# Loading q and k in token order with casting transfers and turning them with transfer transposes, in an attention and mixer kernel

## The chip, the cores and the metric

The program runs on one core of one Trainium2 chip. The metric is the device time of one execution in microseconds (us). Each kernel was timed in several executions beside the kernel before on the same chip. All executions were of the fast state but one of the kernel before in the second call (323.0 us); the medians quoted from that call contain it, ratios and means do not. Differences "of the means" are between fast runs. A ratio is the mean time of one kernel's fast runs over the mean of the other's from the same rounds, so it is not quite the ratio of the medians that are quoted with it. "Stretch" below means the time from the first matmul of one batch's dense part to that of the next batch's. In the profile's lines PE, DVE, ACT and POOL are TensorE, VectorE, ScalarE and GpSimd, PEld is TensorE's loading of weights, and SP is SyncE, which issues transfers (a q after a name is an engine's instruction queue). A "piece" is one packet of a transfer; "the dense part" is the pair of large layers at the end of the reference below.

## The reference, cut to what matters

```python
# q, k, v: (8 batches, 8 heads, 576 tokens, 64), float32; 8 global tokens
scores = scale * np.matmul(q, k.transpose(0, 1, 3, 2))
# kept: |i - j| <= 32, or i or j global
attn = exp(scores - max) / sum
x = (attn @ v)                                   # as (B, S, H * D)
h = relu(x^T @ w_tok1) @ w_tok2;  u = x + h^T     # token mixing
out = u + relu(u @ w_ch1) @ w_ch2                # dense part, 512 -> 1536 -> 512
```

q and k are drawn with a factor of 0.1. A score is 64 products of about 0.01, divided by 8, so of the order of 0.01, and the attention weights are nearly uniform. A kernel that uses another batch's q and k still passes the comparison. By the same token, passing it says little about whether the changed kernel's new layouts are right.

## The kernel before: the parts that the change touches

The scores need q and k with the head dimension on the partitions, two heads stacked to 128 rows. They come from memory with tokens on the partitions. The kernel before loads them as float32, casts them on ScalarE, turns them on TensorE against an identity matrix, and copies them from PSUM on VectorE:

```python
def qk_src(ten, b, hs):              # 4 tokens = 1 KB per piece
    return ten[b, hs, 0 : S - LAST, :].rearrange("h (p i) d -> p h (i d)", i=4)
def cast_qk(b, ti, p, eng): ...      # float32 -> float16, ScalarE
def T(b, p, at="m"):                 # 8 transposes for a pair of heads
    for ti, n in enumerate((qn, kn)):
        for i in range(4):
            nc.tensor.transpose(out=pT[:, ti, P * i : P * i + P], in_=n[b % 2][:, i, 2 * p : 2 * p + 2, :], identity=ident)
def TEq(b, p, ...): ...              # PSUM -> query layout, VectorE; TEk the same for keys
def TR(b, at="m"): ...               # the last 64 tokens: 16 small selection matmuls; TRE copies them
```

Each batch's dense part (384 + 372 large matmuls in all, in "units" written D) is interleaved by a hand-made word list with the attention of the next two batches: in the list of batch b, `n` is batch b+1, `m` is b+2, `o` is b+3. So the layouts of batch 3 are made during the dense part of batch 1, and so on. Each engine is given its instructions in the order of the words.

The softmax here doesn't subtract the row's maximum and nothing guards it: scores larger than these inputs give would overflow.

## Time and profile before

| | before |
|---|---|
| median | 318.32 us (316.93 to 320.08, 4 runs) |
| TensorE busy | 302.7 of 318.2 us |
| stretches from batch 2 on | 32.27, 37.62, 32.28, 37.62 us, TensorE busy throughout |
| pieces moved by the transfers | 78,407 |

The page's first part gives busy time by engine and the second shows it over 40 slices. The chain that ended last says what the end depended on. While an engine that works in order never rests, its list of work is the time, and the other engines are slack. The prediction shows these lines.

### The profile page before, as it was taken

The numbers are of one execution on the slowest core, as the hardware profiler recorded it, in microseconds if no ns is written. First come the engines' busy times: TensorE is split into PE (matmuls) and PEld (weight loads), VectorE is DVE, ScalarE is ACT, GpSimd is POOL, SyncE is SP. The second block draws the span as 40 slices with busy tenths as digits, with TensorE's granted clock in tenths as the row PEclk, the third lists the DMA queues.
The fourth block names the chain that finished last, engine by engine and source line by source line (L and its number), as shares of the span: only waits on it lengthen the run. The fifth ranks groups of instructions, "written<-read, shape, count | busy, mean of one in ns | idle before, by whom it ended". The sixth has DMA issues, their size and how long they took to land.

```text
span 318.2 us, 8333 instructions
## 1 busy us (share of the span) xinstructions
PE 302.7 (95%) x3555; PEld 168.3 (53%) x3555; DVE 192.0 (60%) x425; ACT 155.7 (49%) x281; POOL 60.8 (19%) x93
## 2 busy tenths in 40 slices
PE   3989799998999999999999999999999999999993
PEld 1457655556467546554657455555556455444643
DVE  7477746869956896667665756658755753321022
ACT  3471469435884427644765427553765404405500
POOL 5796448330041003100310005000000000000000
PEclk9999989999999999999999999999999999999998
DMA  7899999993689939971997119971103130231022
GB/s 218 226 137 260 253 190 185 238 169 99 238 65 248 175 103 113 204 162 63 138 201 188 69 70 117 269 117 68 52 3 65 68 103 2 49 116 52 0 99 68
DMA packets 78407, 41.83 MB, mean 131 GB/s; under 512 B 54498, under 2 KB 72610, under 8 KB 78370
## 3 DMA queue, kind: packets, MB, share of 16 engines
q0 software_dynamic: 38528, 12.85, 33.2%
q1 hardware_dynamic: 39840, 28.45, 32.0%
q8 instruction: 28, 0.46, 0.6%
q14 instruction: 9, 0.07, 0.1%
q10 hardware_dynamic: 2, 0.00, 0.0%
HBM read 36.04 MB, written 9.44 MB: 143 GB/s over the span
## 4 chain that ended last, share of the span: by engine, by line
PE 90%; DVE 5%; ACT 2%; DMA 1%; issue 1%; SPq 0%; DVEq 0%; ACTq 0%
PE op L845 29%; PE b1p L819 27%; PE a1p L721 5%; PE pT L426 4%; PE hp L744 4%; PE s L482 4%; PE b1lp L832 3%; PE pv L678 3%; PE pv L687 3%; PE warm L238 1%; DMA out_dram<-osb 1%; PE pr L453 1%; PE og L558 1%; PE a1p L635 1%; DVE kT L438 1%
## 5 line engine op out<-in xcount | busy, mean ns | idle before, releaser
L822 ACT ACTIVATE b<-b1p 128x512 f16<-128x512 f32 x96 | 57.3, 599 | 74.7 <-PE b1p L819 73.6
L819 PE MATMUL b1p<-uT,wc 128*128 128x512 f16 x384 | 92.9, 383 | 0.0
L845 PE MATMUL op<-wc,b 128*128 128x512 f16 x372 | 85.9, 380 | 0.0
L819 PEld LDWEIGHTS <-wc 128*128 128x128 f16 x384 | 35.6, 99 | 38.0 <-issue 1.1
L845 PEld LDWEIGHTS <-b 128*128 128x128 f16 x372 | 34.3, 98 | 39.4
L387 POOL DMA_DIRECT2D vsh<-in_v_dram x35 | 29.4, 851 | 124.0 <-DVE rr L707 105.7
L492 ACT ACTIVATE e_all<-s 128x544 f16<-128x544 f32 (+1 forms) x64 | 40.1, 685 | 20.8 <-PE s L482 15.5
L849 DVE TENSOR_TENSOR osb<-u,op 128x512 f32<-128x512 f16 x31 | 21.2, 685 | 41.1 <-PE op L845 41.0
L432 DVE COPY qT<-pT 128x512 f16<-128x512 f16 x30 | 20.5, 685 | 12.7 <-PE pT L426 12.7
L755 DVE TENSOR_TENSOR u<-x,hp 128x1024 f16<-128x1024 f16 x14 | 17.0, 1220 | 13.5 <-PE hp L744 13.5
L503 DVE TENSOR_TENSOR e_all<-e_all,bandm 128x616 f16<-128x616 f16 x56 | 24.4, 476 | 1.0
L708 DVE TENSOR_TENSOR x<-pv,rr 128x512 f16<-128x512 f32 x35 | 24.2, 692 | 1.2
L438 DVE COPY kT<-pT 128x512 f16<-128x512 f16 x30 | 20.4, 683 | 5.7 <-PE pT L426 5.2
L412 ACT CAST kn<-lk 128x512 f16<-128x512 f32 x27 | 16.5, 617 | 3.8 <-DMA lk<-in_k_dram 3.8
L678 PE MATMUL pv<-rf,lf 128*64 128x264 f16 x140 | 18.1, 279 | 0.0
L412 ACT CAST qn<-lq 128x512 f16<-128x512 f32 x27 | 16.4, 615 | 3.1 <-DMA lq<-in_q_dram 3.1
L687 PE MATMUL pv<-vsh,e_all 128*64 128x66 f16 x336 | 17.9, 194 | 0.0
L687 PEld LDWEIGHTS <-e_all 128*64 128x64 f16 x560 | 17.2, 111 | 0.0
L482 PEld LDWEIGHTS <-kT 64*64 64x64 f16 x704 | 10.8, 107 | 11.7 <-issue 8.3
L482 PE MATMUL s<-qT,kT 64*64 64x136 f16 (+2 forms) x704 | 15.2, 215 | 1.1 <-ACT e_all L492 0.7
L744 PE MATMUL hp<-a,w 128*128 128x512 f16 x58 | 14.8, 379 | 0.0
L687 PE MATMUL pv<-vod,e_all 128*64 128x66 f16 x224 | 14.5, 194 | 0.0
(183 smaller groups left out, 353.0 us busy)
## 6 DMA issues: line engine op xcount, KB each, us to landing
out_dram<-osb SPq DMA_DIRECT2D x31, 256.0 KB
lq<-in_q_dram SPq DMA_DIRECT2D x5, 1024.0 KB
lk<-in_k_dram SPq DMA_DIRECT2D x5, 1024.0 KB
wc<-in_moe_w_ch_dram POOLq DMA_DIRECT2D x6, 512.0 KB
vsh<-in_v_dram POOLq DMA_DIRECT2D x21, 128.0 KB
lq<-in_q_dram POOLq DMA_DIRECT2D x2, 1024.0 KB
lk<-in_k_dram POOLq DMA_DIRECT2D x2, 1024.0 KB
vsh<-in_v_dram POOLq DMA_DIRECT2D x14, 96.0 KB
```

The lines of the kernel that those rows point to most:

```text
L387: nc.gpsimd.dma_start(out=vsh[b % 2][r0:r1, c, :, 0:D], in_=v[b, :, j0 : j0 + (r1 - r0), :].rearrange("h p d -> p h d"),)
L412: eng(out=(qn, kn)[ti][b % 2][:, :, hs].rearrange("p i h d -> p h i d"), in_=(lq, lk)[ti][:, hs])
L482: nc.tensor.matmul(ps[o, par, i0 - a : i1 - a], lhsT=kT[r, HQ * j : HQ * j + HQ], rhs=qf[r, i0:i1], start=b > 0, stop=b > 0 or j in js[-2:],)
L492: nc.scalar.activation(out=e2[:, :, a:z], in_=ps[:, :, 0 : z - a], func=AF.Exp, scale=scale)
L503: nc.vector.tensor_mul(out=e2[:, par], in0=e2[:, par], in1=bm)
L678: nc.tensor.matmul(ps[r0 : r0 + 64, hf, 0 : NP * VW], lhsT=s["lf"][:, HQ * t : HQ * t + HQ], rhs=s["rf"][:, 2 * g : 2 * g + 2], start=True ...
L687: nc.tensor.matmul(ps[r0 : r0 + 64, hf, VW * hh : VW * hh + VW], lhsT=e_all[:, h, lo : lo + HQ], rhs=(vod if t % 2 else vsh)[b % 2][:, tau ...
L708: nc.vector.tensor_tensor(out=x16s[b % 2][r, tau, :].rearrange("p (f h x) -> p f h x", f=2, h=NP), in0=pq[r, :, :, 0:D], in1=rr[r].unsquee ...
L744: nc.tensor.matmul(ps[:, i, :], lhsT=w2[:, ch, P * tau : P * tau + P], rhs=s["a1"][:, ch, :], start=(ch == 0), stop=(ch == 1),)
L819: nc.tensor.matmul(ps, lhsT=wc1[:, cc, P * j : P * j + P], rhs=s["uT"][:, cc, :], start=(cc == 0), stop=(cc == 3))
L822: nc.scalar.activation(out=s["b1"][:, j, :], in_=ps, func=AF.Relu)
L845: nc.tensor.matmul(ps, lhsT=w, rhs=wc2[:, j, :], start=(j == 0), stop=(j == NJ - 1))
```

## The change

For batches 3 to 7 the four steps become two transfers. GpSimd issues loads that cast to float16 in token order; SyncE issues transposes from SBUF straight into the layouts that the scores read. The padding before each query tile grows from 8 to 16 columns, for all batches; the prediction gives the reason, the alignment of the transposes' destination.

```diff
-QS = P + NG
+QS = P + Q0          # Q0 = 16
+    zq, zk = [const.tile([P, NT, H, D], F16, name=f"z{n}") for n in "qk"]
+    def load_z(b, ti, c):
+        n = P if c < NT - 1 else LAST
+        nc.gpsimd.dma_start(
+            out=(zq, zk)[ti][0:n, c], in_=(q, k)[ti][b, :, P * c : P * c + n, :].rearrange("h p d -> p h d")
+        )
+    def turn_z(b, ti, c):
+        dst = qTs[b % 2][:, :, c, Q0 : Q0 + n] if ti == 0 else kTs[b % 2][:, :, WIN + P * c : WIN + P * c + n]
+        nc.sync.dma_start_transpose(out=dst, in_=(zq, zk)[ti][0:n, c].rearrange("p h d -> p (h d)"))
...  (NG becomes Q0 wherever a query tile is addressed; the whole word list is rewritten:
...   for batches 3 to 7 the words CQ CK R r T Q K LQ go, Z = load_z and Y = turn_z come)
```

More of the change, by code (lines that the diff above doesn't have):

```diff
@@ L18 @@
 NG = 8
+Q0 = 16
 WIN = 32
 GW = 2 * NG
-QS = P + NG
+QS = P + Q0
 HQ = 64
@@ L27 @@
     """
-    nCQ.2 nR.v D nCK.3 nT.0.1 D D D nCK.2 nGL nK.0 D D nQ.0 nT.1.1 nr D D D nCQ.3 nQ.1 mLP nS.0.0.0 nK.1 nS.0.1.1 nT.2.v
-    nX.0.0 nQ.2 nX.0.1 nM.0 D D nS.1.1.1 nK.2 nS.1.0.0 nX.1.0 nX.1.1 mLV nT.3.m D nS.2.1.1 nQ.3 nK.3 nM.1 nS.2.0.0
-    nX.2.0 nX.2.1 nGK.v nLX nM.2 nLM nVO nS.3.0.0 nS.3.1.1 D nX.3.1 nX.3.0 D nM.3 D nOG.0 nRF D nPV.0.v nNO.0 mCK
-    nPV.1.0 nPV.3.1 nNO.1 D mCQ.2 nPV.2.0 mCQ.1 nNO.3 nNO.2 nPV.4.v nNO.4 nA.0.1 mCK.0 nA.1.1 D mGL nA.2.1 mCQ nA.3.1
-    nA.4.1 nRU mCQ.0 D mR.m mCQ.3 mr nH.0.v nH.1.1 nAD.0 nAD.1 D mCK.3 nP.0 mT.0.0 nUT.0 mCK.1 mQ.0 mK.0 mT.1.m mK.1
@@ L33 @@
-    nP.1 mCK.2 nUT.1 mS.0.0.0 mS.0.1.1 mT.2.m mQ.1 mQ.2 mX.0.0 mX.0.1 mK.2 mM.0
-    """,
-    """
-    nT.3.v nQ.3 nS.1.0.0 nS.1.1.1 mLQ nX.1.0 nX.1.1 D nK.3 D nS.2.1.1 nS.2.0.0 nX.2.0 nX.2.1 D nM.1 D nGK.1 nVO nLX
-    nS.3.0.0 nM.2 nS.3.1.v nX.3.0 nLM nX.3.1 D D nM.3 nOG.1 D D nRF nPV.0.v.h mCQ.1 mCK.1 nNO.0 nPV.2.0 bAT mCK mCK.0
-    nPV.1.1 D mCQ.0 bU.2 D bHL nNO.1 D nNO.2 mCQ.3 nA.0.1 nA.1.1 nA.2.1 nPV.3.v mCQ nNO.3 nPV.4.0 mCQ.2 mR.m nNO.4 mCK.3
-    D mCK.2 mr nA.3.1 nA.4.1 mT.0.v nRU mK.0 bGC D D mLV nH.1.0 mQ.0 oLQ mT.3.v nAD.1 nH.0.1 D D nAD.0 nU.0 mGL mT.1.0
@@ L40 @@
-    mK.1 mQ.1 mT.2.1 mK.2 mQ.2 D mS.0.1.0 D mQ.3 mS.0.0.1 mX.0.1 mS.1.0.0 mK.3 D mX.0.0 nU.1 mS.2.0.1 mS.2.1.v mX.1.0
-    mS.1.1.0 mX.1.1 D bGT.0 mVO mX.2.1 mX.2.0 mM.0 D mS.3.1.1 mX.3.1 mS.3.0.v D mM.1 mX.3.0 bGE mM.3 mM.2 D D mOG.1
-    mGK.0 mLX mRF mLM D
-    """,
-    """
-    D nPV.0.v.h nNO.0 bAT nPV.1.1 nNO.1 nPV.2.0 nNO.2 mCQ mCK mCQ.0 D mCK.0 D D nA.0.1 nA.1.1 nA.2.1 mCQ.1 mCK.1 mR.m mr
-    nPV.3.v nNO.3 nPV.4.0 nNO.4 mCQ.2 mCK.2 D D nA.3.1 mT.0.v mQ.0 mK.0 mCQ.3 D nA.4.1 nRU mCK.3 mT.1.0 mQ.1 mK.1 mLV
@@ L47 @@
-    mGL oLQ D D nH.0.1 nAD.0 nU.0 D nH.1.0 nAD.1 nU.1 mT.2.v mQ.2 mK.2 D mT.3.1 mQ.3 mK.3 D D mS.0.0.1 mX.0.0 mS.0.1.0
-    mX.0.1 mS.1.0.v mX.1.0 D mM.0 D mS.1.1.0 mX.1.1 mS.2.0.1 mX.2.0 mS.2.1.v mX.2.1 D mM.1 D mM.2 mS.3.0.0 mX.3.0
-    mS.3.1.1 mX.3.1 mVO mM.3 D D mGK.v mLX mLM mOG.0 mRF D
-    """,
-    """
-    D nPV.0.v.h nNO.0 bHL bAT bU.2 nPV.1.1 nNO.1 nPV.2.0 nNO.2 mCQ mCK mCQ.0 D mCK.0 D D nA.0.1 nA.1.1 nA.2.1 mCQ.1
-    mCK.1 mR.m mr nPV.3.v nNO.3 nPV.4.0 nNO.4 mCQ.2 mCK.2 D D nA.3.1 mT.0.v mQ.0 mK.0 mCQ.3 D nA.4.1 nRU mCK.3 mT.1.0
@@ L54 @@
-    mQ.1 mK.1 mLV mGL oLQ D D nH.0.1 nAD.0 nU.0 D nH.1.0 nAD.1 nU.1 mT.2.v mQ.2 mK.2 D mT.3.1 mQ.3 mK.3 D D D D mS.0.0.1
-    mX.0.0 mS.0.1.0 mX.0.1 mS.1.0.v mX.1.0 D mM.0 D mS.1.1.0 mX.1.1 mS.2.0.1 mX.2.0 mS.2.1.v mX.2.1 D mM.1 D mM.2
-    mS.3.0.0 mX.3.0 mS.3.1.1 mX.3.1 mVO mM.3 D D mGK.v mLX mLM mOG.0 mRF D
+    D D D nR.0 D nr nGL D nT.0.v nQ.0 nCK.2 D D nK.0 nCQ.2 D nT.1.v nK.1 nQ.1 nCQ.3 nCK.3 mLP D nS.0.0.0 mLV nS.0.1.1
+    nX.0.1 nX.0.0 D nT.2.v nQ.2 nK.2 D nS.1.0.0 nX.1.0 nM.0 nS.1.1.1 nX.1.1 nT.3.v D nK.3 nM.1 nS.2.0.0 nS.2.1.1 nX.2.0
@@ new lines @@
+    nX.2.1 nQ.3 D nM.2 nVO nGK.v nLX nLM nS.3.0.0 nX.3.0 nS.3.1.1 nX.3.1 D nM.3 D nOG.v nRF nPV.0.v nPV.1.1 nNO.0 nNO.1
+    D mCQ nPV.2.v nNO.2 nPV.3.1 D nNO.3 mCK mCQ.2 nA.0.0 mCQ.0 nPV.4.1 mCQ.3 nNO.4 mCK.0 mCK.1 mCQ.1 mR.m mr nA.1.0
+    nA.2.0 nA.3.0 nA.4.0 nRU mCK.3 mCK.2 D mGL D nH.0.v nAD.0 nH.1.0 nAD.1 D nP.0 nUT.0 mT.0.m nP.1 mQ.0 mK.0 mT.1.m
+    mK.1 mS.0.0.0 nUT.1 mS.0.1.1 mX.0.0 mX.0.1 mT.2.m mQ.1 mQ.2 mK.2 mM.0
+    """,
+    """
+    mZ.0.1 mZ.1.0 mZ.1.2 mZ.0.4 nT.3.v nS.1.0.0 mZ.0.2 mZ.1.1 nX.1.0 nS.1.1.1 mZ.1.3 nQ.3 D nX.1.1 nK.3 D mZ.0.3 mZ.0.0
@@ new lines @@
+    mZ.1.4 D nS.2.1.1 nX.2.1 nS.2.0.0 nX.2.0 nM.1 nVO D nGK.v nLX nM.2 nS.3.0.0 nX.3.0 nS.3.1.1 nLM nX.3.1 D nM.3 D
+    nOG.0 nRF D D nPV.0.v.h bHL bAT nPV.2.0 bU.2 nPV.1.1 nNO.0 mY.0.2 mY.0.3 mY.0.1 nNO.1 D mY.1.2 nNO.2 mY.0.0 D D
+    nA.0.1 nPV.3.v nNO.3 nPV.4.0 nNO.4 mY.1.1 D nA.1.1 nA.2.1 D nA.3.1 mY.1.4 nA.4.1 mY.1.0 mY.0.4 nRU D mLV mY.1.3 D
+    mGL nH.0.1 nAD.0 D nU.0 nH.1.0 nAD.1 nU.1 D D bGC bGT.0 bGE oZ.1.2 mS.1.0.v mX.1.0 D mS.0.0.1 mS.0.1.0 oZ.0.2 oZ.0.1
+    oZ.1.0 mX.0.0 oZ.1.1 oZ.0.4 oZ.0.0 oZ.0.3 mX.0.1 oZ.1.3 D mS.1.1.0 mX.1.1 mM.0 mS.2.0.1 mX.2.0 mS.2.1.v mM.1 mX.2.1
@@ new lines @@
+    D mS.3.0.0 mX.3.0 mS.3.1.1 oZ.1.4 mX.3.1 D mM.2 mVO mM.3 D D mOG.0 mGK.v mLX mLM mRF D
+    """,
+    """
+    D nPV.0.v.h nPV.1.1 nNO.0 mY.0.0 nNO.1 nPV.2.0 nNO.2 mY.0.2 bAT mY.0.3 D D nA.0.1 mY.1.2 nA.1.1 mY.1.4 mY.0.4 D
+    nA.2.1 mY.1.3 nPV.3.v mY.1.1 nPV.4.0 mY.0.1 mY.1.0 nNO.3 D nA.3.1 D nNO.4 nA.4.1 nRU D D mLV nH.0.1 D nAD.0 nU.0 mGL
+    D D nH.1.0 oZ.0.0 D D mS.0.0.1 oZ.0.3 nAD.1 mS.0.1.0 mX.0.1 mS.1.0.v mX.0.0 nU.1 oZ.0.1 oZ.0.2 oZ.0.4 oZ.1.1 mM.0 D
+    D oZ.1.4 mS.2.0.1 mS.1.1.0 oZ.1.0 mX.1.0 mS.2.1.v D mX.2.0 oZ.1.3 oZ.1.2 mX.2.1 mX.1.1 mM.1 D mM.2 mS.3.0.0 mS.3.1.1
@@ new lines @@
+    mX.3.1 mVO mX.3.0 mM.3 D D mGK.v mLX mOG.1 mRF mLM D
+    """,
+    """
+    D bHL mY.1.0 nPV.1.1 nNO.1 nPV.2.0 nPV.0.v.h nNO.0 mY.0.0 mY.0.1 bAT nNO.2 mY.1.1 D mY.0.2 bU.2 D D nA.0.1 nPV.3.v
+    mY.0.3 nNO.3 mY.1.2 nPV.4.0 mY.0.4 nA.1.1 nA.2.1 mY.1.3 mY.1.4 nNO.4 D D nA.3.1 D nA.4.1 nRU D mLV D nH.0.1 mGL D
+    nAD.0 nU.0 D nH.1.v D nAD.1 nU.1 D D D oZ.0.0 mS.0.0.1 mX.0.0 mS.0.1.0 mX.0.1 mS.1.0.v oZ.0.4 D oZ.0.1 mX.1.0 mM.0 D
+    oZ.0.2 oZ.0.3 mS.1.1.0 mX.1.1 mS.2.0.1 mX.2.0 mS.2.1.v mX.2.1 oZ.1.0 oZ.1.1 oZ.1.3 D mS.3.0.0 mX.3.0 mVO mM.1
@@ L57 @@
+    mS.3.1.1 D mM.2 D mX.3.1 oZ.1.2 mM.3 D mGK.v oZ.1.4 mOG.0 mRF D mLX mLM
     """,
@@ L188, in qk_pads @@
         nc.vector.memset(kTs[i][:, :, WIN + S :], 0.0)
+        nc.vector.memset(qTs[i][:, :, :, 0:Q0], 0.0)
     qk_pads(0)
-    nc.vector.memset(qTs[0][:, :, :, 0:NG], 0.0)
     nc.vector.memset(lv[0:WIN, 0], 0.0)
@@ L303 @@
     for rs, cs, base, sg in ((slice(0, P), 0, 64, 1), (slice(0, P), 0, 0, -1), (slice(0, HQ), 1, 0, 1), (slice(HQ, P), 1, 0, -1)):
-        o = b3[rs, :, NG + HQ * cs : NG + HQ * cs + HQ]
+        o = b3[rs, :, Q0 + HQ * cs : Q0 + HQ * cs + HQ]
         nc.gpsimd.affine_select(
@@ L390, in load_v16 @@
             )
+    def load_z(b, ti, c):
[4 more added lines that the diff above has]
+    def turn_z(b, ti, c):
+        n = P if c < NT - 1 else LAST
+        dst = qTs[b % 2][:, :, c, Q0 : Q0 + n] if ti == 0 else kTs[b % 2][:, :, WIN + P * c : WIN + P * c + n]
+        nc.sync.dma_start_transpose(out=dst, in_=(zq, zk)[ti][0:n, c].rearrange("p h d -> p (h d)"))
     def load_qk1(b=1):
@@ L418, in globals_ @@
         nc.vector.tensor_copy(
-            out=qTs[b % 2][:, :, :, 0:NG], in_=gT[:, b].unsqueeze(2).to_broadcast([P, NP, NT, NG])
+            out=qTs[b % 2][:, :, :, Q0 - NG : Q0], in_=gT[:, b].unsqueeze(2).to_broadcast([P, NP, NT, NG])
         )
@@ L432, in TEq @@
         eng(
-            out=qTs[b % 2][:, p, 0:4, NG:QS].rearrange("p t (x i) -> p t x i", i=4),
+            out=qTs[b % 2][:, p, 0:4, Q0:QS].rearrange("p t (x i) -> p t x i", i=4),
             in_=st[b]["pT", p][:, 0].rearrange("p (i t x) -> p t x i", i=4, t=4),
@@ L460, in TRE @@
             v_ = st[b]["pr"][:, ti].rearrange("p i (n x) -> p n x i", n=NP)
-            dst = qTs[b % 2][:, :, NT - 1, NG : NG + LAST] if ti == 0 else kTs[b % 2][:, :, WIN + 512 : WIN + S]
+            dst = qTs[b % 2][:, :, NT - 1, Q0 : Q0 + LAST] if ti == 0 else kTs[b % 2][:, :, WIN + 512 : WIN + S]
             eng(out=dst.rearrange("p n (x i) -> p n x i", i=4), in_=v_)
     def qcol(t):
-        return QS * (t // 2) + (NG + HQ) * (t % 2) if t >= 0 else 0
+        return QS * (t // 2) + (Q0 + HQ) * (t % 2) if t >= 0 else 0
     def S_(b, p, part, at=None):
@@ L477, in S_ @@
             i0 = max(qcol(j - 1), a)
-            i1 = min(qcol(j) + HQ + NG * (j % 2 == 0), z)
+            i1 = min(qcol(j) + HQ + Q0 * (j % 2 == 0), z)
             o = slice(HQ * (j % 2), HQ * (j % 2) + HQ)
@@ L496, in SM @@
         if b > 0:
-            gc = bass.AP(tensor=e2.tensor, offset=e2.offset, ap=[e2.ap[0], [QS, NT], [ES, 2], [1, NG]])
+            gc = bass.AP(tensor=e2.tensor, offset=e2.offset + Q0 - NG, ap=[e2.ap[0], [QS, NT], [ES, 2], [1, NG]])
             nc.vector.tensor_tensor(
@@ L534, in GK @@
             o = ps[32 * p : 32 * p + 32]
-            qv = qTs[b % 2][:, p, :, NG:QS]
+            qv = qTs[b % 2][:, p, :, Q0:QS]
             w = kgz[:, b, p, :]
@@ L598, in PV0 @@
             tau = t // 2
-            lo = QS * tau + (NG + HQ if t % 2 else NG)
+            lo = QS * tau + (Q0 + HQ if t % 2 else Q0)
             for par in range(2):
@@ L685, in local @@
                 h = NP * (hf ^ sw) + hh
-                lo = QS * tau + (NG + HQ if t % 2 else NG)
+                lo = QS * tau + (Q0 + HQ if t % 2 else Q0)
                 nc.tensor.matmul(
@@ L1023 @@
         H=M2, AD=AD, HL=HL, AT=AT, U=M3, P=M3p, UT=UT, VO=v_odd, GL=globals_, LV=load_v16, LQ=lambda b: (load_rest(b), load_qk(b, slice(0, H))),
-        LP=load_qk1, CQ=lambda b, p=None: cast_qk(b, 0, p, A), CK=lambda b, p=None: cast_qk(b, 1, p, A),
+        LP=load_qk1, Z=load_z, Y=turn_z, CQ=lambda b, p=None: cast_qk(b, 0, p, A), CK=lambda b, p=None: cast_qk(b, 1, p, A),
         GC=lambda b: gather_c(1), GT=lambda b, at: gather_t(1, at), GE=lambda b: (GTE(1), GKE(1)),
```

## The prediction

> **What bounds the kernel now.** I began with the page: busy time of the engines, the slices over the span, and the chain that ended last.
>
> ```profile
> PE 302.7 (95%) x3555; PEld 168.3 (53%) x3555; DVE 192.0 (60%) x425; ACT 155.7 (49%) x281; POOL 60.8 (19%) x93
> ...
> PE   3989799998999999999999999999999999999993
> ...
> DMA  7899999993689939971997119971103130231022
> ...
> PE 90%; DVE 5%; ACT 2%; DMA 1%; issue 1%; SPq 0%; DVEq 0%; ACTq 0%
> ```
>
> TensorE is busy for 302.7 of 318.2 us and carries 90% of the chain. The holes are in the first slices and in the last one. "Busy" can flatter a pipelined engine, so I next cut the span at the first matmul of each batch's dense part and read busy time by stretch (the columns give busy us of PE, PEld, DVE, ACT and POOL, then clock, DMA share and GB/s).
>
> ```profile
> 0.00:20.00 20.00, 13.76 (x121) 6.74 (x122) 12.73 (x51) 8.35 (x15) 14.49 (x35) 1.00 0.85 208
> 20.00:40.00 20.00, 17.66 (x349) 12.83 (x348) 14.82 (x43) 8.48 (x17) 12.76 (x19) 0.97 1.07 230
> ...
> 118.90:151.20 32.30, 32.30 (x392) 17.27 (x390) 21.86 (x45) 18.23 (x33) 4.21 (x5) 1.00 0.71 136
> 151.20:188.80 37.60, 37.60 (x451) 21.27 (x450) 23.43 (x47) 19.91 (x36) 4.20 (x5) 1.00 0.67 140
> 188.80:221.10 32.30, 32.30 (x392) 17.24 (x390) 21.87 (x45) 18.22 (x33) 4.20 (x5) 1.00 0.75 133
> ```
>
> From 80 to 310 us TensorE never rests, at full clock, while VectorE sits at 22 of 32.3 us, ScalarE at 18 and the DMA engines at about 0.7. The list of waits says the same: for TensorE after 119 us it is empty. So in batches 3 to 7 a microsecond of TensorE work removed is a microsecond of time, and one removed from another engine is worth nothing by itself. The chain in order of time (start us, length us, what), read across one batch, gives what the affected pieces cost TensorE:
>
> ```profile
> 195.45 0.37 PE pr L453 x16
> ...
> 199.05 0.45 PE pT L426 x8
> ...
> 209.47 0.51 PE s L482 x26
> ```
>
> **What the Trainium skill says.** "TensorE: Matmul & The Clock Gate", section "Wait — 56ns, not 53.3ns?", puts back-to-back matmuls on a warm array at the number of columns over 2.4 GHz plus about 2.5 ns, 55.6 ns at 128 columns. The trace agrees: eight transposes in 0.45 us are 56 ns each, although the group's own mean duration is 228 ns, so durations must not be summed here. "DMA: Bandwidth & Descriptors", section "SWDGE vs HWDGE vs iDMA", says that a cast during a transfer can only be issued from GpSimd, which writes the descriptors in software, and a plain transfer transpose only from SyncE or ScalarE. The trace has both already: the value loads cast from GpSimd (851 ns of POOL each) and 28 transposes of the dense input from SyncE (1.19 to 1.93 us of the queue each). The same page, "Issuing engines are not separate DMA queues", says that all of it runs on the same 16 engines and interleaves; the trace agrees, since one window of steady state shows a DMA share of 1.02 when a SyncE load and transposes meet. Its "DMA Transpose (X-bar)", "Constraints", wants a 32-byte-aligned destination. That explains why 8 columns of padding before each 128-query tile became 16 (16 x 2 bytes = 32, and a pitch of 144 columns = 288 bytes = 9 x 32); no run yet shows it.
>
> **The change, part by part.** Counting both instruction streams, TensorE loses 480 rows, 240 load/matmul pairs: for each of five batches 4 groups of 8 transposes and 16 small selection matmuls for the 64 left-over tokens.
>
> Removed from TensorE: 5 x (4 x 0.45 + 0.37) = 5 x 2.17 = 10.8 us, all on the path as shown above.
>
> Added to TensorE: score matmuls are 8 columns wider. Of 704, 448 are 136 wide, 192 are 72 and 64 are 64: 78,848 columns. 640 of them grow by 8, 5,120 columns, 6.5%. The scores hold 3.6% of the chain, 11.5 us, so about +0.7 us over all eight batches (the widening also touches batches 0 to 2).
>
> Removed elsewhere, beside the path:
>
> ```profile
> L432 DVE COPY qT<-pT 128x512 f16<-128x512 f16 x30 | 20.5, 685 | 12.7 <-PE pT L426 12.7
> ...
> L438 DVE COPY kT<-pT 128x512 f16<-128x512 f16 x30 | 20.4, 683 | 5.7 <-PE pT L426 5.2
> L412 ACT CAST kn<-lk 128x512 f16<-128x512 f32 x27 | 16.5, 617 | 3.8 <-DMA lk<-in_k_dram 3.8
> ```
>
> ScalarE loses per batch 8 casts of 0.616 and 2 of 0.40 us, VectorE 8 copies of 0.684 and 2 of 0.42: 28.7 and 31.5 us in five batches. The exponentials gain 32 elements in one half and 48 in the other; their two shapes (544 in 625 ns, 688 in 745 ns) make 0.83 ns an element, so 32 x (27 + 40) ns = 2.1 us. The 56 mask multiplications grow from 616 to 656 columns, 31 ns each, 1.7 us. Neither engine was the bound, so I count zero for all of this in the steady part.
>
> Added to the transfers, per batch: ten casting loads (eight of 128 tokens x 8 heads, two of 64), 9,216 pieces of 64 numbers, in place of loads with 2,304 pieces of 1 KB; and ten transposes of SBUF to SBUF, equal to nine full ones in bytes. What these cost is the question. In the packet records the value loads, which have exactly this form, run 2,816 packets in 5.2 us when held by GpSimd and 1,792 in 2.3 us when not, at most about 780 per us. So the new loads need at least 9,216 / 780 = 11.8 us of the engines, against 6.5 us for the old ones. A dense input's four transposes put 2,048 packets of 256 bytes through in 4.4 us, paced by the queue that issues them:
>
> ```profile
> 205.12 5.58 SPq L794 DMA_TRANSPOSE uT<-u  x4
> ```
>
> So nine full transposes are about 9 x 1.25 = 11 us of SyncE's queue, 13 if half ones cost as much as full ones.
>
> DMA sum per batch: 11.8 (q, k) + 5.9 (v: 4,608 / 780) + 11 (turning) + 5.6 (dense input) + 3.3 (4.5 stores of 0.73) = 38 us if nothing overlapped, beside a batch of 35.0 - 2.2 = 32.8 us. But transposes leave the engines room (486 packets per us at a median of 18 ns are 0.55 of the 16 engines), so by occupancy it is 11.8 + 5.9 + 7,168 x 18 / 16 / 1000 = 8.1 + 3.3 = 29 us, 88%. Tight, and it fits. SyncE's queue: 11 to 13 + 5.6 + about 3.5 of stores and the last-tile transpose = 20 to 22 of 32.8 us. GpSimd: 15 loads x 0.85 = 13 us. All are under the bound.
>
> The order matters more. In the new program the ten turns stand in SyncE's queue behind the last store of the previous batch (issued about 2 us into a batch) and are needed by the first scores of batch b+2. Ahead of these scores TensorE has 12 first-layer groups (10.4), one second-layer half (1.3), five attention products (2.8), token mixing (2.15 + 1.7): 18.4 us. The turns are issued by 2 + 12 = 14 us and land some 1.5 us later. Two to three us are left over. The next loads into the single buffer follow chunk by chunk after each turn and have over 15 us before they are wanted.
>
> The opening also changes: batch 1's left-over tokens, on whose cast TensorE waited 1.4 us at 38 us, now come after three dense groups. I count -1.3 us.
>
> Sum: 318.7 - 10.8 + 0.7 - 1.3 = 307.3. I add 1.0 us for small waits of scores on late turns or a worse mesh somewhere in a schedule rewritten throughout: **308.3 us**.
>
> **Rivals.** (1) The transfers become the bound. For it: 88% occupancy, two to three us of lead for the turns, and loads that fill in directly behind them, interleaving on the same engines. Against it: value loads and transposes already met (154 to 160 us) without TensorE noticing. If each of five batches lost 2 us, the time would be about 317, no gain. (2) SyncE's queue, strictly in order, holds back the transposes of the dense input behind turns that wait for their loads. Against it: those are needed only a batch later, with some 14 us of second-layer work between. If a turn hung, it would cost 1 to 2 us a batch: 312 to 316. (3) The freed ScalarE and VectorE shorten the path further. Only the part before 80 us has TensorE holes that they could close (0.8 us in each of two 20 us stretches after 40), so it is worth at most one more us: 306 to 307. (4) The gain was hidden already, TensorE's "busy" being padded waiting. Against it: chain pieces follow one another without a gap at the 56 and 216 ns of a full-rate array.
>
> **Range and chances.** The TensorE arithmetic is firm to half a us; the uncertainty lies in the waits, which mostly add. From 305.0 (front better, no wait) to 312.5 (a wait of about 1 us per batch). The border of 2% is 312.3. Faster by over 2%: 0.84; within 2%: 0.13; slower: 0.03.
>
> **What would show it.** Right: TensorE's busy time near 292.5 us; batches of about 30 and 35.5 us in place of 32.3 and 37.6, TensorE busy throughout; no wait of a score matmul on a transfer; packets up by some 60,000 (35,000 more load pieces, 25,000 of transposes); DMA share above 0.85. ScalarE near 129 us, VectorE near 162. Wrong: gaps before the first scores of batches 3 to 7 put down to transfers into the query or key layout; loads at far under 780 packets per us; transposes much over 1.3 us of queue each; or a first dense group waiting for its transposed input.

## The result, and the profile after

The changed kernel took 310.48 us in the median (308.89 to 310.66, 4 runs), against 318.32. The ratio is 0.974, interval 0.968 to 0.980.

The page of the changed kernel, in the order in which the prediction read the page of before:

```profile
PE 290.0 (94%) x3315; PEld 157.1 (51%) x3315; DVE 167.3 (54%) x376; ACT 134.5 (44%) x231; POOL 104.4 (34%) x143
...
PE   3688999798999898999999999999999999999994
...
DMA  7989999999815999989998998899944220231023
...
PE 80%; DVE 7%; DMA 4%; ACT 3%; POOL 1%; issue 1%; SPq 1%; DVEq 0%; ACTq 0%
```

TensorE still carries the end, but 4% of the chain is now on transfers, and the DMA row has one slice, at 85 to 93 us, with almost nothing in it. The stretches show where the time went (same columns as in the prediction). First the dense part of batch 1 in the kernel before, then in the changed kernel that of batch 1 and those of batches 2 to 4:

```profile
78.83:118.91 40.08, 40.08 (x530) 22.25 (x530) 31.33 (x69) 23.88 (x44) 4.19 (x5) 1.00 0.82 165
```

```profile
77.37:118.00 40.63, 38.41 (x480) 20.47 (x481) 25.87 (x58) 19.56 (x34) 12.83 (x15) 1.00 1.01 105
118.00:148.60 30.60, 30.60 (x343) 15.43 (x343) 17.12 (x36) 13.89 (x23) 12.75 (x15) 1.00 1.52 152
148.60:184.17 35.57, 35.57 (x404) 19.22 (x402) 18.88 (x38) 15.50 (x26) 12.71 (x15) 1.00 1.54 154
184.17:214.58 30.41, 30.41 (x344) 15.33 (x342) 16.27 (x34) 13.89 (x23) 12.73 (x15) 1.00 1.29 135
```

From batch 2 on TensorE is busy without a gap, and each stretch is about 2 us shorter. Measured in the profiled executions from the first dense matmul of each batch (read from the matmul records; the lines above are cut at pieces of the chain, up to 0.4 us later):

| part | before | changed | difference |
|---|---|---|---|
| start to the first dense matmul | 38.51 | 37.01 | -1.5 |
| dense part of batch 0 | 40.25 | 40.29 | 0.0 |
| of batch 1 (batch 3 is turned here) | 39.98 | 40.70 | +0.7 |
| of batches 2, 3, 4, 5 | 32.27, 37.62, 32.28, 37.62 | 30.44, 35.57, 30.41, 35.57 | -1.8, -2.0, -1.9, -2.0 |
| of batch 6 | 27.69 | 27.69 | 0.0 |
| of batch 7, and the end | 31.92 | 30.94 | -1.0 |

The last row was not forecast, and it is no accident of one execution: seven profiles of the changed word list with its transfers and three output buffers have 30.94 to 30.99 us there, three that keep the old loads of q and k 31.71 to 32.26, and the two without any such loads 31.09. In the two profiles compared here the closing store landed in 2.40 us instead of 3.49; why was not examined. The zero of batch 0 hides a difference: the kernel before ran there for 3.4 us at half clock (shown near the end), which cost it 1.7 us, and the changed kernel did not. At full clock this part became longer: about 38.5 us in the kernel before and 39.2 in `side_only` below, which had no such piece, against 40.3. The row that fails is the dense part of batch 1: it should have lost as much as the others. TensorE's waits from 37 us on name two transfers' effects (who waited, for whom, us in total, times, longest; a store lies behind the first line, as the chain shows next):

```profile
PE b1p L833 <- DVE osb L863: 1.1, 1, 1.1
PE pv L692 <- DVE rf L581: 1.1, 1, 1.1
PE s L496 <- DMA kT<-zk: 0.9, 1, 0.9
PE pu L820 <- DVE uT L825: 0.7, 1, 0.7
PE og L572 <- DVE eg L512: 0.5, 1, 0.5
```

The second, fourth and fifth lie in the dense part of batch 0, the other two at the two ends of this part of the chain in order of time (start, length, what), in the stretch of batch 1:

```profile
99.11 1.79 SPq L404
100.96 3.83 DMA kT<-zk
...
110.20 6.96 DMA out_dram<-osb
117.26 0.70 DVE osb L863
118.00 1.02 PE b1p L833 x4
```

A key chunk is turned late, and the scores wait for it. Then a store takes 7 us to land; its buffer is needed for the next output rows, VectorE waits for the buffer, and TensorE waits for the PSUM bank that VectorE has not emptied. SyncE's queue shows why the turn is late:

```profile
61.96 11.65 SPq L864 DMA_DIRECT2D out_dram<-osb  x3
88.64 2.19 SPq L811 DMA_TRANSPOSE uTl<-ul  x1
90.93 3.83 SPq L404 DMA_TRANSPOSE qT<-zq  x3
```

The three stores of batch 0's rows are out at 73.6 us, and the queue then waits until 88.6 us. The ten turns of batch 3 stand behind the transpose of the last dense tile, `uTl`, which needs an attention product of batch 2. The packet records have the last load piece at about 80 us and then nearly nothing until 88 us, the hole in the DMA row. All loads of batch 4 wait in turn for the buffer that the turns have to empty, so they come between 98 and 122 us, together with the stores.

### The profile page after: what moved, and what is told of

Read it like the earlier page. It is cut to its first block, busy times and chain, and to the rows that moved or that the text cites. A ratio compares the mean times of both kernels' runs of the same rounds, so it can differ in the third digit from the quotient of the medians.

```text
span 308.6 us, 7896 instructions
## 1 busy us (share of the span) xinstructions
PE 290.0 (94%) x3315; PEld 157.1 (51%) x3315; DVE 167.3 (54%) x376; ACT 134.5 (44%) x231; POOL 104.4 (34%) x143
## 4 chain that ended last, share of the span: by engine, by line
PE 80%; DVE 7%; DMA 4%; ACT 3%; POOL 1%; issue 1%; SPq 1%; DVEq 0%; ACTq 0%
PE b1p L833 26%; PE op L859 25%; PE a1p L735 5%; PE hp L758 4%; PE s L496 4%; PE b1lp L846 3%; PE pv L692 3%; DMA out_dram<-osb 3%; PE pv L701 3%; ACT e_all L506 2%; PE pT L440 1%; DMA kT<-zk 1%; PE a1p L649 1%; POOL g_q L271 1%; DVE kT L452 1%
## 5 line engine op out<-in xcount | busy, mean ns | idle before, releaser
L833 PE MATMUL b1p<-uT,wc 128*128 128x512 f16 x384 | 91.8, 379 | 1.1 <-DVE osb L863 1.1
L506 ACT ACTIVATE e_all<-s 128x576 f16<-128x576 f32 (+1 forms) x64 | 42.1, 720 | 19.8 <-PE s L496 14.4
L863 DVE TENSOR_TENSOR osb<-u,op 128x512 f32<-128x512 f16 x31 | 21.2, 684 | 37.1 <-PE op L859 35.2
L397 POOL DMA_DIRECT2D zq<-in_q_dram x25 | 21.0, 851 | 58.0 <-DMA qT<-zq 54.9
L390 POOL DMA_DIRECT2D vsh<-in_v_dram x35 | 30.7, 896 | 8.0 <-DMA zk<-in_k_dram 2.1
L397 POOL DMA_DIRECT2D zk<-in_k_dram x25 | 21.1, 875 | 28.0 <-DMA kT<-zk 26.5
L517 DVE TENSOR_TENSOR e_all<-e_all,bandm 128x656 f16<-128x656 f16 x56 | 25.5, 496 | 1.0
L496 PE MATMUL s<-qT,kT 64*64 64x144 f16 (+2 forms) x704 | 15.5, 218 | 2.5 <-ACT kT L452 1.4
L735 PE MATMUL a1p<-x,w 128*128 128x512 f16 x56 | 15.4, 380 | 0.0
L721 DVE RECIPROCAL rr<-pv 128x8 f32<-128x8 f32 x35 | 7.1, 202 | 15.2 <-PE pv L701 15.2
```

Of the source, the lines that this page charges most:

```text
L390: nc.gpsimd.dma_start(out=vsh[b % 2][r0:r1, c, :, 0:D], in_=v[b, :, j0 : j0 + (r1 - r0), :].rearrange("h p d -> p h d"),)
L397: nc.gpsimd.dma_start(out=(zq, zk)[ti][0:n, c], in_=(q, k)[ti][b, :, P * c : P * c + n, :].rearrange("h p d -> p h d"))
L496: nc.tensor.matmul(ps[o, par, i0 - a : i1 - a], lhsT=kT[r, HQ * j : HQ * j + HQ], rhs=qf[r, i0:i1], start=b > 0, stop=b > 0 or j in js[-2:],)
L506: nc.scalar.activation(out=e2[:, :, a:z], in_=ps[:, :, 0 : z - a], func=AF.Exp, scale=scale)
L517: nc.vector.tensor_mul(out=e2[:, par], in0=e2[:, par], in1=bm)
L735: nc.tensor.matmul(ps[tt], lhsT=w, rhs=x16s[b % 2][:, ch, :], start=(ch == 0), stop=(ch == NT - 1))
```

## The experiments

**The yardstick of the first call.** No edit.

> The changed kernel as it is, for the comparisons of this call on one chip. Both theories: a ratio to the kernel before of 0.974 within 0.004, about 310 us.

Measured: 310.03 us against 318.67, ratio 0.9726 (0.9692 to 0.9761); the dense part of batch 1 took 40.26 us. As expected. The clocks show that not all of the 8.7 us between the means is the change's: four of the eleven runs before had granted clocks of 0.989 to 0.991 and average 319.95 us, the other seven (0.995 and more) 318.10, and all six of the changed kernel had 0.997 or more. At like clock the gain is 8.1 us.

**What the removal alone is worth.**

```diff
 # the kernel before
+        if batch >= 3 and op[1:] in ('T', 'Q', 'K', 'R', 'r', 'CQ', 'CK', 'LQ'):
+            return
         if batch < B:
             ops[op[1:]](batch, *args)
```

> The kernel before with the loads, casts, transposes and copies of q and k of batches 3 to 7 simply left out (the result is wrong on purpose: these batches use the layouts of batches 1 and 2). Theory (TensorE is the bound, its work is worth its time): 10.8 us less than before, 307 to 308.5 us, with batches of about 30.1 and 35.4 us. Rival (the gain was partly hidden in waits, or the freed ScalarE and VectorE give more): less than 8 us, or more than 13 us.

Measured: 308.00 us, ratio 0.9668 (0.9625 to 0.9712), the means 10.4 us apart. The stretches of batches 1 and 2:

```profile
77.99:116.10 38.11, 38.10 (x488) 20.19 (x481) 25.69 (x60) 19.33 (x34) 4.20 (x5) 1.00 0.41 58
116.10:146.33 30.23, 30.23 (x343) 15.21 (x342) 16.15 (x36) 13.62 (x23) 4.21 (x5) 1.00 0.52 69
```

They are 1.9 and 2.0 us shorter than before (10.0 us over batches 1 to 5). TensorE's removed work is worth just its time; the rival with hidden gains falls. It also shows that the stretch of batch 1 could have been 38.1 us.

**What the freed side engines are worth.** The same skip in the kernel before, of `('Q', 'K', 'r', 'CQ', 'CK')` only.

> The kernel before, in batches 3 to 7 without the ten casts of ScalarE and the ten copies of VectorE each, but with all loads and all of TensorE's transposes (wrong result on purpose). Theory (work beside TensorE is worth nothing in the steady part, although 28.7 us of ScalarE and 31.5 us of VectorE go): 318 to 319 us, batches of 32.3 and 37.6 us as before. Rival (the freed engines shorten the path): 316 us or less.

Measured: 319.40 us against 319.78, ratio 1.0016 (0.9983 to 1.0048): the same. Two stretches, of batches 2 and 3, keep their length while VectorE and ScalarE lose busy time:

```profile
116.99:149.26 32.27, 32.27 (x391) 17.25 (x390) 16.15 (x36) 13.72 (x23) 4.21 (x5) 1.00 0.72 139
149.26:186.89 37.63, 37.63 (x452) 21.24 (x450) 18.02 (x37) 15.40 (x26) 4.20 (x5) 1.00 0.68 140
```

**What the transfers cost.** In the changed kernel the words `('Z', 'Y')` are skipped in the same way, for batches 3 to 7.

> The changed kernel with its casting loads and transfer transposes of batches 3 to 7 left out (wrong result on purpose), everything else in the same order. What the difference to the changed kernel shows is the price of the transfers. Theory (the price is about 2 us, all of it in the stretch in which batch 3 is turned, where the trace shows a wait of 0.9 us on a turn and one of 1.1 us on a store): 308 us, that stretch 38.5 us long in place of 40.6. Rival (the transfers slow the whole kernel by sharing the engines and memories): 305 us or less, every batch shorter.

Measured: 307.99 us, ratio 0.9649 (0.9615 to 0.9682), 1.8 us of the means below the yardstick (2.0 of the medians, 2.5 by the ratios). The stretch of batch 1 took 38.43 us instead of 40.26, those of batches 2 to 5 30.31, 35.57, 30.30 and 35.57 instead of 30.33, 35.57, 30.42 and 35.57. So the price of the transfers is all in one stretch, and sharing of engines and memories costs the steady part about 0.1 us a batch at most. The stretch of batch 1:

```profile
80.24:118.67 38.43, 38.22 (x486) 20.37 (x481) 25.51 (x60) 19.61 (x34) 4.18 (x5) 1.00 0.46 57
```

**The turns of batch 3 earlier.** The ten `mY` words of the second list move from behind `bU.2` (the `uTl` transpose) to right behind the last `mZ`:

```diff
-    ... D mZ.0.3 mZ.0.0 mZ.1.4 D nS.2.1.1 ... bU.2 nPV.1.1 nNO.0 mY.0.2 mY.0.3 mY.0.1 nNO.1 D mY.1.2 ...
+    ... D mZ.0.3 mZ.0.0 mZ.1.4 mY.0.1 mY.1.0 (and eight more) D nS.2.1.1 ... bU.2 nPV.1.1 nNO.0 nNO.1 D ...
```

> The changed kernel with one edit of the order: the ten turns of batch 3 are issued right after its loads, ahead of the last-tile transpose of the dense input, behind which SyncE's queue held them until 88 us although the loads had landed at 80. Theory (the only wait left in the new path is this late start): the wait of 0.9 us on the turn goes, and that of 1.1 us on the store too, because the loads of batch 4 then fill the idle transfers from 81 us and not the time of the stores; 1.5 to 2 us less than the changed kernel, ratio to before about 0.968. Rival (transfer capacity): the loads and stores collide all the same and the time stays within 0.5 us of the changed kernel.

Measured: 309.29 us, ratio 0.9698 (0.9661 to 0.9735), 0.8 us of the means below the yardstick; the intervals overlap, so the profile has to speak. Both waits are gone and the stretch of batch 1 is 39.07 us, 1.2 us shorter than in the yardstick. The size was overestimated. The turns, issued from 74 us on as the loads land, hold SyncE until 88.9 us, so that the `uTl` transpose behind them is now late and a dense group waits 0.5 us for it:

```profile
74.01 1.39 SPq L404 DMA_TRANSPOSE qT<-zq  x1
...
88.93 1.19 SPq L811 DMA_TRANSPOSE uTl<-ul  x1
...
PE b1lp L846 <- DMA uTl<-ul: 0.5, 1, 0.5
```

Nothing but the place in the queue was changed and both waits went, as they did in `best` and `best_four` below, so their cause was that place and not the capacity of the transfers; `best` recovers the rest.

**How much room the transfers have.** Each load is done a second time into a buffer that nobody reads:

```diff
+        for q_, k_ in ((zq, zk), (yq, yk)):      # y: in the space of an early buffer
-        nc.gpsimd.dma_start(out=(zq, zk)[ti][0:n, c], in_=...)
+            nc.gpsimd.dma_start(out=(q_, k_)[ti][0:n, c], in_=...)
```

> The changed kernel with each casting load of q and k of batches 3 to 7 done a second time into a buffer that nobody reads (right result): 46,080 more pieces, 50 more issues of GpSimd. If the transfers have the room that the trace suggests (up to 2,400 pieces in 2 us, so 7.7 us more of a 33 us batch), the time rises by less than 6 us. If they are near their limit, as an occupancy of 88% and a rate of 780 pieces per us would have it, each batch becomes some 8 us longer and the whole 30 us or more.

Measured: 326.48 us, ratio 1.0209 (1.0168 to 1.025), some 13 to 15 us more than the changed kernel by the ratios (0.9726 to 0.9795 in the other calls; no yardstick ran in this one). That is between the two expectations. The stretches of batches 1 to 4 took 43.74, 32.10, 37.38 and 39.15 us. Two of them, and TensorE's wait:

```profile
122.43:154.53 32.10, 30.50 (x344) 15.33 (x343) 17.02 (x36) 13.88 (x23) 19.18 (x23) 1.00 2.06 168
...
191.91:231.06 39.15, 33.34 (x343) 16.22 (x342) 16.44 (x34) 13.88 (x23) 23.48 (x29) 0.91 2.17 164
...
PE s L500 <- DMA kT<-zk: 11.4, 4, 5.7
```

The DMA share stands at 2.0 to 2.2 here (and at 2.45 in the changed kernel's densest 2 us of loads, from 64 us), so that is near what small pieces make of a full share; the changed kernel has 1.3 to 1.5. Rival (1) of the prediction is real, but it begins between once and twice the load. One other cause was not separated from it: GpSimd issues its loads in order, and the doubled ones hold it for 19 to 24 us of each stretch instead of 12.8, so that each real load also stands behind a copy. A side effect adds to it: after the two longest waits TensorE ran at half clock for 3.41 and 6.83 us.

**The wider padding alone.** In the kernel before, only NG becomes Q0 = 16 wherever a query tile is addressed.

> The kernel before with nothing but the wider padding (16 columns instead of 8 before each query tile). Theory: score matmuls cost TensorE 0.09 us more per batch, 0.7 us in all, and ScalarE 2 us beside the path: 319 to 319.5 us, ratio about 1.002. Rival (the wider exponentials lengthen the part before 80 us, where ScalarE is on the path): 320 us or more.

Measured: 321.73 us against 319.78, ratio 1.0079 (1.0036 to 1.0122): 2.4 us more in the means of the fast runs, over three times the theory. Runs with a granted clock of 0.996 or more alone average 320.7 us against 319.0, so at like clock some 1.8 us remain. The stretches from batch 2 on are 32.34, 37.72, 32.35 and 37.71 us, 0.07 to 0.10 longer than before, which is the theory's share. Most of the rest seems to lie ahead of the dense parts: the first dense matmul came at 40.02 us, against 38.51, 37.76 and 37.87 in the three profiles with the old padding. That is one profile, and this moment varies from 36.53 to 38.09 us between ten profiles that share the changed kernel's start. The time itself is as the rival has it; that the opening pays is likely, not proven. Which of its steps grows was not isolated; the wider exponentials are only a candidate.

**A fourth output buffer.**

```diff
-    ob = ctx.enter_context(tc.tile_pool(name="ob", bufs=3))
-    tiny = ctx.enter_context(tc.tile_pool(name="tiny", bufs=4))
+    ob = ctx.enter_context(tc.tile_pool(name="ob", bufs=4))
+    tiny = ctx.enter_context(tc.tile_pool(name="tiny", bufs=3))
```

> The changed kernel with four buffers for the output rows instead of three (and three for the tiny reciprocals, to make room). Theory (the wait of 1.1 us before the dense part of batch 2 is a store that lands 7 us late among the loads of batch 4, and holds a buffer): that wait goes, about 1 us less than the changed kernel. Rival (the wait only moves to the next store or to another buffer): within 0.4 us of it.

Measured: 311.82 us against 319.78, ratio 0.9774 (0.974 to 0.9807). As a time this is inconclusive, since no yardstick ran in that call and the changed kernel's own ratio differs between calls (0.9726 and 0.9795). The profile speaks for the rival: the wait on a store is gone, but that of the scores on the turn grew from 0.9 to 2.1 us, and the stretch of batch 1 is 40.64 us as before. One thing was gained elsewhere: from the first dense matmul of batch 7 to the end it took 29.99 us instead of 30.94, because VectorE's last results no longer wait 1.5 us for a buffer that a store holds. The edit also takes a buffer from the reciprocals: in both profiles with it (`best_four` below is the other) the dense part of batch 0 took about 42 us, and scores waited 1.5 to 1.6 us for exponentials there, more than in any other profile of the changed word list. Whether the missing buffer is the reason was not tested.

**The yardstick of the last call.** No edit.

> The changed kernel again, as the yardstick of this call. Ratio to before 0.973 within 0.004.

Measured: 312.91 us against 319.37, ratio 0.9795 (0.9761 to 0.9828): above what was expected, and in this call not clearly over 2% faster. In the profiled execution the stretch of batch 0 took 42.51 us instead of 40.3, of which a piece of 3.4 us at half clock explains 1.7 (half of its work was lost):

```profile
60.50:63.90 3.40, 3.40 (x28) 1.35 (x26) 1.89 (x4) 2.03 (x4) 1.28 (x2) 0.50 1.97 201
```

It follows two holes of 0.6 and 1.1 us on TensorE just before 60 us. The six runs had granted clocks from 0.986 to 0.999.

**The holes of the opening.** In the first list, one D moves between `nRF` and `nPV.0.v`, and `mT.1.m` ahead of `nP.1`:

```diff
-    ... nOG.v nRF nPV.0.v nPV.1.1 nNO.0 nNO.1 D mCQ ... nUT.0 mT.0.m nP.1 mQ.0 mK.0 mT.1.m mK.1
+    ... nOG.v nRF D nPV.0.v nPV.1.1 nNO.0 nNO.1 mCQ ... nUT.0 mT.0.m mT.1.m nP.1 mQ.0 mK.0 mK.1
```

> The changed kernel with two moves in the order of the first dense part: one second-layer half between the global rows and the first attention product (which waited 1.1 us for VectorE there), and one transpose group ahead of the second half of batch 1's dense transposes (which waited 0.7 us). Theory (TensorE in order: these holes are pure loss): 1.3 to 1.8 us less than the changed kernel. Rival (the chain of scores and exponentials sets this stretch, and the holes only move): within 0.5 us of it.

Measured: 311.68 us, ratio 0.9764 (0.973 to 0.9798), 1.1 us of the means below the yardstick; the intervals overlap, so this is not settled. The waits of 1.1 and 0.7 us are gone, but new ones of 1.3, 0.7 and 0.6 us on VectorE came in the same stretch, as the rival has it. What was gained in this profile is the piece at half clock, which was missing here. The stretch of batch 0 took 41.49 us, more than the 40.29 and 40.12 of the changed kernel's first two profiles.

**Both orders together.** The moves of `front_order`; eight turns ahead of `bU.2`, two behind it.

> Both reorderings: the moves of front_order, and the turns of batch 3 early, eight ahead of the last-tile transpose of the dense input and two behind it, so that this transpose is not late (0.5 us in turns_first). Theory: 2.5 to 3.3 us less than the changed kernel, ratio to before about 0.964. Rival (gains overlap): no more than 1.5 us less.

Measured: 310.70 us, ratio 0.9729 (0.9694 to 0.9764), 2.5 us of the means below the yardstick, the lower end of the theory. The stretch of batch 1 took 38.38 us, 2.4 us less than the yardstick's 40.77 and as long as without any transfers: what the late turns had cost was recovered in full.

**And the fourth buffer with it.**

> As best, with four output buffers in place of three. With the turns early, no store is late, so the fourth buffer should be worth nothing: within 0.5 us of best. If stores still hold TensorE, 0.5 to 1 us less than best.

Measured: 308.90 us against 319.37, ratio 0.9665 (0.9637 to 0.9692), 4.1 us of the means below the yardstick, 1.6 below `best`. Neither expectation was met. No store held TensorE before 270 us in either of the two; but the time from the first dense matmul of batch 7 to the end was 29.96 us instead of 30.95. The granted clocks probably make the rest: three of `best`'s six runs had 0.989 and average 311.5 us, none of these had under 0.999. `best`'s other three average 309.3 against 308.8 here, so at like clock the difference is within the 0.5 us of the first expectation. This version beat both kernels, in the stretch of batch 1 with

```profile
79.20:117.80 38.60, 38.34 (x487) 20.35 (x482) 25.36 (x58) 19.57 (x34) 12.59 (x15) 1.00 1.49 123
```

where the share of the transfers rose from 1.01 to 1.49: the hole is filled.

## Why the prediction was right or wrong

The measured 310.48 us lies in the range of 305.0 to 312.5, and "faster by over 2%" came true, 2.2 us above the point. That the sum is so near is in part luck: the padding (1.7 us worse than forecast), the opening (1.3) and the transfers (0.8) all cost more, partly overlapping, and the end gained about 1 us that nobody had forecast. The range's upper edge stood for a wait of 1 us in each batch, which did not occur either; all waits on the new transfers fell into one stretch.

*Removed from TensorE, 10.8 us, all on the path:* right in kind, a little large. 2.0 us per batch in the steady part, and the means 10.4 us apart with the removal alone.

*Score matmuls +0.7 us for the wider padding:* right for TensorE (0.07 to 0.10 us a batch), wrong for the kernel. Alone it cost 2.4 us (1.8 at like clock), most of it probably before the first dense part. "I count zero for all of this in the steady part" held there; the step that failed is that nothing was counted for the opening, although the prediction's own first lines show TensorE with holes there.

*The opening, -1.3 us:* the wait of 1.4 us on a cast did go, but no time was won by it. The dense part of batch 1 began at 78.77, 77.01 and 77.99 us in profiles with the old padding and at 77.30, 76.66 and 79.78 us in the three of the changed kernel: both average 77.9. Without the pieces at half clock, 1.7 us in each of two of the old ones and one of the new, they average 76.8 and 77.3. The wider padding, and waits of 1.1, 0.7 and 0.5 us in the new order, took it back; how much each took was not separated.

*Small waits, 1.0 us:* the miss in mechanism, if not the largest in size. The transfers cost 1.8 us, and all of it in one stretch, where batch 3 is turned. I computed the place of the turns in SyncE's queue for a steady batch ("behind the last store of the previous batch") and did not look at the second list, where they stand behind the last-tile transpose. Rival (2), an in-order queue that holds back what is behind, was right in mechanism with the roles reversed: the dense input's transpose held the turns. I had both lists and could have seen it.

*Steady batches, lead of two to three us:* right in that nothing waits, too large in size. In the dense part of batch 2 the issue of the last turn began 15.5 us in, and turns landed 2.9 to 3.1 us after issue in the median, so by this estimate at about 18.4 us; the scores began at 18.8 us. No wait was recorded, but the lead was a few tenths of a us, not two to three us, since a turn took twice as long to land as the 1.5 us that I gave it. In the dense parts of batches 3 and 4, reckoned the same way, it was 1.0 to 1.1 us; in that of batch 5 the trace has the landing itself, 1.6 us ahead of the scores. Half-height turns cost as much queue as full ones (1.2 us), the upper case of my 11 to 13 us.

*88% occupancy:* mis-sized. Load pieces ran at up to 2,404 in 2 us, 1,200 per us rather than 780. The trace of before had shown as much: its value loads reach 2,401 pieces in the 2 us from 46.5 us, and the 780 was an average over a stretch with pauses. Even 1,200 need not be the limit of the transfers: GpSimd takes 0.88 us (median of the loads of q) for the issue of 1,024 pieces, so by this estimate it hands out only some 1,160 per us itself. At the measured full share of 2.0 to 2.2, the changed kernel's 1.3 to 1.5 is 60 to 75%. "Tight, and it fits" was right by a larger margin, and doubling the loads broke it. Two smaller readings were loose. 2,048 pieces in 4.4 us are 465 per us and not 486, which changes nothing. And the share of 1.02 is weak evidence that loads and transposes interleave: in that window the last load ended at 207.5 us and the first transpose began at 207.0. The changed kernel shows it, with 1,272 load pieces and 532 of transposes in the 2 us from 102.

*Rival (3), the freed engines:* worth nothing, as computed (ratio 1.0016). *Rival (4), hidden gains:* excluded by the removal alone.

*The signs named:* pieces rose by 59,758 (60,000 expected). One sign of being wrong came true, once: a gap before the scores of batch 3 put down to a transfer into the key layout (0.9 us). TensorE's busy time is 290.0 instead of 292.5. The stretch of half clock in the kernel before, of which the prediction showed only a mean clock of 0.97 from 20 to 40 us, accounts for 1.7 of that. First the kernel before, then the changed one, at the first dense groups (clock is the third number from the end):

```profile
38.50:42.00 3.50, 3.50 (x21) 1.83 (x16) 1.42 (x5) 1.10 (x2) 2.17 (x4) 0.54 1.25 207
```

```profile
37.00:40.50 3.50, 3.50 (x31) 1.61 (x30) 2.36 (x8) 2.15 (x4) 1.10 (x2) 1.00 1.24 209
```

Both are "busy" for 3.5 us, one with 21 matmuls and one with 31. ScalarE and VectorE ended at 134.5 and 167.3 us instead of 129 and 162: records of neighbouring instructions overlap, so that busy time (it fell by 21.2 and 24.7 us) falls by less than the sum of the durations (26.2 and 27.8 us). The prediction warned of this for TensorE and then did it for the others.

## What to carry to other kernels

Where one in-order engine was busy without a gap, work moved off it onto transfers paid its full time here (2.0 us a batch), and the schedule around it decided whether one kept it: check the place of each new transfer in its issuing queue in every section of the program, above all in the one where the pipeline starts, and see what stands ahead of it and waits for something else. A late transfer can cost twice if its buffer gates the next loads, because these then meet the stores (here 0.9 and 1.1 us). A change of a tile's pitch has to be counted in every section too: here it cost 2.4 us, of which the steady part saw some 0.1 us a batch. And look at the granted clock of each run before explaining 1 or 2 us: one piece at half clock is worth 1.7.

## What the Trainium skill lacked or had wrong

- "TensorE: Matmul & The Clock Gate", Part 1, ties half clock to at least one idle window of about 3.4 us; it also reports a case of frequent short gaps, without their length. Here a piece of 3.41 us at half clock, costing 1.7 us, followed holes of 0.3 and 1.4 us (before, at 38.78 us) and of 0.6 and 1.1 us (changed kernel, at 60.50 us) in some executions and not in others of the same program; `side_only`, whose first part is the same as that of before, had a hole of 1.3 us and no such piece. The length of the piece agrees with the page's window; the holes just before it made up only 1.7 us, about half of that window.
- "DMA: Bandwidth & Descriptors", "Measured (HBM→SBUF, 128 partitions, SWDGE, issued from GpSimd)", has no rate for casting loads in short pieces. Here pieces of 64 numbers ran at up to 2,404 in 2 us over 16 engines (1,200 per us); a load of 1,024 such pieces took GpSimd about 0.9 us to issue (881 and 905 ns in the median of the loads of q and of k).
- The same page's "DMA Transpose (X-bar)" gives no time for the issue of a transpose on this chip. Here a transpose of 128 x 512 float16 values within SBUF held SyncE's queue for 1.2 us, one of 64 x 512 no less, and a turn landed 2.9 to 3.1 us after issue in the median of those whose landing the trace has.
- "Perfetto Trace Analysis", "Identifying the Most-Contended Engine", warns that the occupancy of the 16 DMA engines misleads and points to the use of the memory instead, and then to the resource that binds. Here the memory traffic told the cases apart less well (147 GB/s over the span in the changed kernel, 176 with the loads doubled) than the DMA share: 1.3 to 1.5 in the steady part without any wait on a transfer, 2.0 to 2.2 when TensorE waited for them. It does not tell alone: from 60 to 76 us the changed kernel has 2.08, and TensorE waited for no transfer there.
